# Linear attention into an MLP mixer on one core: every engine's order after the first batch taken from one written list

## The chip, the core and the metric

The kernel runs on one core of a Trainium2 chip. The core has a matrix engine (TensorE, PE in the profile, its weight loads PEld), three engines for elementwise work (VectorE or DVE, ScalarE or ACT, GpSimd or POOL) and SyncE (SP), which here only issues transfers. Every engine works off its own queue of instructions strictly in order; an instruction that waits holds up all that stands behind it on that engine, and nothing else. The metric is the device time of one execution in microseconds (us), lower is better.

## The reference

For each of 8 batches (8 heads, 576 positions, head size 64), attention without softmax, then a mixer over tokens and over channels:

```python
q_p, k_p = (phi(q), phi(k))                    # phi(x) = x + 1 for x > 0, else exp(x)
kv = np.einsum('bhsd,bhse->bhde', k_p, v)
z = np.sum(k_p, axis=2)
num = np.einsum('bhsd,bhde->bhse', q_p, kv)
den = np.einsum('bhsd,bhd->bhs', q_p, z)[..., None] + 1e-06
x = (num / den)                                # heads side by side: [batch, 576, 512]
h = np.maximum(xt @ w_tok1, 0.0) @ w_tok2      # xt: x with tokens last; 576 -> 256 -> 576
u = x + h.transpose(0, 2, 1)
out = u + np.maximum(u @ w_ch1, 0.0) @ w_ch2   # 512 -> 1536 -> 512
```

## The kernel before, in words

A batch's 576 positions are four blocks of 128 and a tail of 64. Operands are bf16, sums are kept in PSUM, eight banks of 128 x 512 f32. A batch n passes through these steps; the names in brackets are those that the changed kernel gives them, with the batch's number in front.

- SyncE loads q, k and v in halves (Lq0 to Lv1). phi takes three instructions a half: exp on ACT (kx, qx), the linear branch on DVE (ka, qa), the minimum of both on DVE (kb, qb). v is cast on ACT, in two halves of the first batches (1v0, 2v1) on DVE (v0, v1).
- TensorE forms kv (K); ACT copies it out (Kc0, Kc1). phi(q) is transposed, in batch 1 by TensorE (Q00 to Q11 with copies Qc), later by a transposing transfer on SyncE's queue (qT0, qT1). TensorE forms numerators and denominators (n); DVE divides (nd, ne, n0 to n2, o0, o1) into x.
- The token mixer is two matmuls (f0, f1 with ReLU on ACT; g0, g1 with the addition of x on DVE, gu0 and gu1). Its result u is transposed by a transfer (uT0, uT1), in batch 0 by TensorE (transposes of `utr_first`, copies on ACT and DVE).
- The channel mixer's first matmul has 12 chunks of the 1536 columns (m0 to m11, in batches 0 and 1 in halves ma and mb), each read out with ReLU (r). In batches 2 to 6 four of the 12 chunks, in batch 7 all, are done in seven products in place of eight (x21 to x27; y reads them), which needs sums of weight blocks (G21 to G24 in `swc`) and of u's blocks (s1 to s4).
- The second matmul is done in seven products too, for two halves of the positions each (p10 to p71), from row sums on DVE (w1 to w4) and weight sums (ws on GpSimd, wt on DVE); ACT holds partial results (c0 to c2), DVE adds u (eW to eZ), GpSimd adds the held parts (hY, hZ, hW) and issues the output's transfers (o). Batch 0 uses plain matmuls for it (q0 to q11, read by z). The tails of 64 positions go in pairs (gt, ut, T, U, V, W; in the last pair c, t and ts).

What sets the order before: the code walks through a list of TensorE pieces per batch (`big`), and a second list (`fill`) says after which piece which other step of this or of the following batches is emitted. The position in that emission is the position in the engine's queue. PSUM banks come from two rings in the first batch and from fixed numbers after it; output rows are staged in `obuf` by a running pointer (`o_slots`). Loads of later batches are held back by explicit waits: `load_all` passes the last transposing transfer as a gate.

Lines that matter below: L543 is the channel mixer's first matmul, L852 and L768 are the second one's products, L583 batch 0's second one, L712 and L740 the seven-product form of the first, L191 kv, L261 the numerators, L312 and L325 the token mixer, L202 TensorE's transposes of phi(q), L503 its transposes of batch 0's u, L521 and L526 the transposing transfers of u and of its tails, L157 and L165 phi on DVE, L176 the casts of v, L642 the weight sums on GpSimd, L700 the sums in `swc`, L610 the read of a tail's output, L861 and L863 the additions of u and of the held parts, L867 the output's transfers, L957 the load of `w_ch1` in four quarters of 384 columns (three chunks each), L798 and L834 the last batch's outputs.

In the first batch TensorE's pieces stand like this before:

```python
    utr_first([0], act)
    utr_first([1], dve)
    mm2_first(1, [2, 3])
    for mc in range(2):
        mm3(0, mc, range(0, 2))
    utr_first([2], act)
    utr_first([3], dve)
    for mc in range(2, 4):
        mm3(0, mc, range(0, 2))
```

Of the kernel before, what the change touches and what calls it, by code (L numbers as in the profile page):

```python
# [10 lines left out]
FP32 = mybir.dt.float32  # L11
# [4 lines left out]
EPS = 1e-6  # L16


@with_exitstack
def kernel(  # L20
# [20 lines left out]
    nc = tc.nc  # L41
# [22 lines left out]
    ring = {1: 0, 2: 0}  # L64

    def bank(at=None):
        if at is None:
            at, ring[1] = ring[1], (ring[1] + 1) % 4
        return psum[:, at]

    def banks(at=None):
        if at is None:
            at, ring[2] = 4 + ring[2], (ring[2] + 2) % 4
        return psum[:, at:at + 2]

    def two16():
        return banks().bitcast(BF16).rearrange("p a (t s) -> p a t s", s=128)
# [24 lines left out]
    uTj = [t.rearrange("p r j c -> p (r j c)").rearrange("p (j r c) -> p j r c", j=NDM, r=R) for t in uT]  # L102
    uTt = const("uTt", [128, 2, NDM, 128])
    cr = [const(f"cr{b}", [128, NCH, SM]) for b in range(2)]
    crt = const("crt", [128, NCH, 128])
    obuf = const("obuf", [128, 8, DM], FP32)
    swc = const("swc", [128, 4, 2, 256])
# [31 lines left out]

    live = {}  # L140
    o_at = [0]

    def o_slots(m):
        at = o_at[0] if o_at[0] + m <= 8 else 0
        o_at[0] = (at + m) % 8
        return obuf[:, at:at + m]

    def phi_exp(nm, n, j0, nj):
        f = raw[nm, rb(n)][:, j0:j0 + nj].rearrange("p j f -> p (j f)")
        e = work.tile([128, 2 * TD], BF16, name="e", tag="e", bufs=4)[:, :nj * TD]  # L150
        nc.scalar.activation(out=e, in_=f, func=AF.Exp)  # L151
        live["e", nm, n, j0] = e

    def phi_add(nm, n, j0, nj):
        f = raw[nm, rb(n)][:, j0:j0 + nj].rearrange("p j f -> p (j f)")
        y = work.tile([128, 2 * TD], BF16, name="y", tag="y")[:, :nj * TD]
        nc.vector.tensor_scalar(out=y, in0=f, scalar1=1.0, scalar2=1.0, op0=ALU.add, op1=ALU.max)  # L157
        for j in range(nj):
            live["y", j0 + j] = y[:, j * TD:]

    def phi_end(nm, n, j0, nj):
        c, i = divmod(j0, 2)
        dst = (kp if nm == "k" else qp)[:, c, :, i:i + nj]
        e, y = live["e", nm, n, j0], live["y", j0][:, :nj * TD]
        live["phi"] = nc.vector.tensor_tensor(  # L165
            out=dst.transpose([0, 2, 1, 3]), in0=e.rearrange("p (i t d) -> p i t d", i=nj, t=T),
            in1=y.rearrange("p (i t d) -> p i t d", i=nj, t=T), op=ALU.min)

    def phi(nm, n, c):
        phi_exp(nm, n, 2 * c, 2)  # L170
        phi_add(nm, n, 2 * c, 2)
        phi_end(nm, n, 2 * c, 2)

    def vcast(n, c, copy=nc.scalar.copy):
        js = slice(2 * c, 2 * c + 2)
        copy(out=vs[:, js, :, 0:D],  # L176
             in_=raw["v", rb(n)][:, js].rearrange("p j (t d) -> p j t d", t=T))

    def bank16():
        return bank().bitcast(BF16).rearrange("p (t s) -> p t s", s=128)  # L180
# [3 lines left out]
    def kv(n, cs):  # L184
        b = n % 2
        ps = banks(4 if n > 1 else None)[:, :, 0:2 * D1].rearrange(
            "p a (c e) -> p a c e", c=2)
        for c in cs:
            for t in range(T):
                for a, i in QUARTERS:  # L190
                    nc.tensor.matmul(out=ps[half[i], a, c], lhsT=kp[half[a], c, t, i],  # L191
                                     rhs=vs[half[a], 2 * c + i, t],
                                     start=(t == 0), stop=(t == T - 1))
        cs = slice(cs[0], cs[-1] + 1)
        for i in range(2):
            at = slice(i * D1, (i + 1) * D1)
            nc.scalar.copy(out=kvbd[b][half[i], cs, :, at].transpose([0, 2, 1, 3]),
                           in_=ps[half[i], :, cs])
# [6 lines left out]
    TS = [range(0, 5), range(5, T)]  # L205

    def qtr_put(n, c, ts, tp, put, dst=None):
        v_ = (qT[n % 2] if dst is None else dst)[:, 0:4 * TD].rearrange("p (a c t s) -> p a c t s", a=2, c=2, t=T)
        put(out=v_[:, :, c, ts[0]:ts[-1] + 1].transpose([0, 2, 1, 3]),
            in_=tp[:, 0:len(ts)].rearrange("p t (a s) -> p t a s", a=2))  # L210

    def qtr(n, c, put=nc.scalar.copy):
        tp = two16()
        for h, ts in enumerate(TS):
            qtr_mm(c, ts, tp[:, h])
        for h, ts in enumerate(TS):
            qtr_put(n, c, ts, tp[:, h], put)

    def qtr_dma(n, halves=range(2)):
        for a in halves:  # L220
            live["crossbar"] = nc.sync.dma_start_transpose(
                out=qT[n % 2][:, 2 * TD * a:2 * TD * (a + 1)].rearrange("p (f s) -> p f s", s=D),
                in_=qp[half[a]].rearrange("p c t i d -> p (c t i d)"))

    def nd_mm(n, c, rs):
        b = n % 2
        ps = banks()
        for s_, r in enumerate(rs):
# [5 lines left out]
        live["nd", c, rs[0]] = ps  # L234

    def nd_end(n, g, rs):
        b = n % 2
        m = len(rs)
        v_ = live["nd", g, rs[0]][:, 0:m, 0:HG * D1].rearrange("p r (h e) -> p r h e", h=HG)
# [9 lines left out]

    def nd_all(n):
        b = n % 2
        ps = [psum[:, 2 + 2 * m:4 + 2 * m] for m in range(3)]
# [10 lines left out]
        xv = x[b].rearrange("p r (c i a d) -> p i (r c) a d", c=2, i=2, a=2)  # L265
        v_ = [ps[m][:, :, 0:D1 * 7].rearrange("p i (k e) -> p i k e", k=7) for m in range(3)]
        dens = work.tile([128, 2, 2, 7], FP32, name="dens", tag="dens", bufs=1)
        last = work.tile([128, 2, 6], FP32, name="dens2", tag="dens2", bufs=1)
        both = psum[:, 2:6, 0:D1 * 7].rearrange("p b (k e) -> p b k e", k=7)
# [4 lines left out]
        def six(m, k0, rc0):  # L274
            den = (dens[:, m] if m < 2 else last)[:, :, k0:k0 + 6]
            nc.vector.tensor_tensor(  # L276
                out=xv[:, :, rc0:rc0 + 3],
                in0=v_[m][:, :, k0:k0 + 6, 0:D].rearrange("p i (q a) d -> p i q a d", a=2),
                in1=den.rearrange("p i (q a) -> p i q a", a=2)[
                    :, :, :, :, None].to_broadcast([128, 2, 3, 2, D]), op=ALU.mult)  # L280

        for m, at in enumerate((6, 0)):
            six(m, m, 4 * m)
            nc.vector.tensor_tensor(
                out=xv[:, :, 3, m], in0=v_[m][:, :, at, 0:D],
                in1=dens[:, m, :, at, None].to_broadcast([128, 2, D]), op=ALU.mult)
        nc.vector.tensor_scalar(out=last, in0=v_[2][:, :, 0:6, D], scalar1=EPS, scalar2=None,
                                op0=ALU.add)
        nc.vector.reciprocal(out=last, in_=last)
        six(2, 0, 7)  # L290

    def nd(n, g, rs):
        nd_mm(n, g, rs)
        nd_end(n, g, rs)

    ALL = slice(0, DM)
# [9 lines left out]
    def mm1(n):  # L306
        b = n % 2
        ps = banks(4 if n > 1 else None)
        for mt in range(NT):
            ms = slice(128 * mt, 128 * mt + 128)  # L310
            for r in range(R1):
                nc.tensor.matmul(out=ps[:, mt], lhsT=w1t[:, b, ms] if r == R else w1[:, r, ms],  # L312
                                 rhs=x[b][:, r, :], start=(r == 0), stop=(r == R))
        for mt in range(NT):
            nc.scalar.activation(out=ar[b][:, mt, :], in_=ps[:, mt], func=AF.Relu)

    def mm2(n, rs, add=False):

        b = n % 2
        m = len(rs)  # L320
        ps = bank().rearrange("p (a d) -> p a d", a=1) if n == 1 else banks(
            None if n < 2 else 4 if rs[0] else 6)
        for i, r in enumerate(rs):
            for kt in range(NT):
                nc.tensor.matmul(out=ps[:, i], lhsT=w2v(kt, r, b),  # L325
                                 rhs=ar[b][:, kt, :], start=(kt == 0),
                                 stop=(kt == NT - 1 and not add))
            if add:
                nc.tensor.matmul(out=ps[:, i], lhsT=identity, rhs=x[b][:, r, :], start=False,
                                 stop=True)  # L330
        if rs[0] == R:
            h = half[b]
            nc.vector.tensor_tensor(out=ut[n // 2 % 2][h], in0=ps[h, 0], in1=x[b][h, R], op=ALU.add)
        elif add:
            nc.scalar.copy(out=u[b][:, rs[0]:rs[0] + m], in_=ps[:, 0:m])
        else:
            nc.vector.tensor_tensor(out=u[b][:, rs[0]:rs[0] + m], in0=ps[:, 0:m],  # L337
                                    in1=x[b][:, rs[0]:rs[0] + m], op=ALU.add)

    def mm2_tails(p):  # L340

        ps = banks(6)[:, 0]
        for kt in range(NT):
            at = D * (T * kt + 2 * R)
# [966 lines left out]
```

## Time and profile before

| what | value |
|---|---|
| timed runs | 247.61 us median of 3 (247.29 to 248.21) |
| profiled execution, first to last instruction (span) | 246.4 us |
| profiled execution, its own time | not listed apart from the timed runs |
| TensorE busy | 236.1 us (96%) |
| VectorE busy | 198.8 us (81%) |
| ScalarE busy | 139.3 us (57%) |
| GpSimd busy | 76.9 us (31%) |
| TensorE clock granted | full in all 40 slices |
| transfers | 48.40 MB |

A busy share is an average over the span. For one step the question is which wait of TensorE ended last there, which the views of waits, of the chain and of the timeline tell. A row's duration is longer than the distance between two such rows that follow each other directly, since the engines overlap the end of one with the start of the next: 379 ns is the mean row of L543, and eight of them take 1.73 us in the chain, 0.216 us each.

### The profile page before, as it was taken

The page shows a single profiled execution, that of the slowest core. Times are in us where ns is not written, and L with a number is a line of the kernel's source. Part 1 is how long each engine was busy: PE and PEld are TensorE (multiplying, and loading weights), DVE is VectorE, ACT ScalarE, POOL GpSimd, SP SyncE. Part 2 cuts the span into 40 slices and gives each one's busy share as a digit, 9 for nine tenths or more (in the row PEclk, how much of TensorE's full clock was granted, in tenths as well). Part 3 has the DMA queues.
Part 4 walks back from the last instruction along what each step waited for, and adds up shares of the span by engine and source line. Part 5 has one row for each costly group of instructions (what it writes and reads, how often), then busy time and mean ns, then how long its engine had stood idle before and what let it go on. Part 6 is the DMA issues. An engine that isn't in the chain of part 4 may idle for free.

```text
span 246.4 us, 6090 instructions
## 1 busy us (share of the span) xinstructions
PE 236.1 (96%) x2477; PEld 162.3 (66%) x2496; DVE 198.8 (81%) x349; ACT 139.3 (57%) x224; POOL 76.9 (31%) x88
## 2 busy tenths in 40 slices
PE   7789999999999899999999999999999999999993
PEld 3475455564868456865678556865676567888883
DVE  5955877889799998988894499979996779956973
ACT  4673881569774367736897167656852652175100
POOL 9670030296703600061004500071007700440360
PEclk9999999999999999999999999999999999999999
DMA  6999999999726796589979955459748702352055
GB/s 248 267 203 258 348 275 308 355 251 289 294 24 133 223 334 271 132 224 210 358 263 174 412 148 192 93 115 329 228 89 94 170 3 43 64 112 61 4 127 130
DMA packets 50444, 48.40 MB, mean 196 GB/s; under 512 B 30192, under 2 KB 36720, under 8 KB 50416
## 3 DMA queue, kind: packets, MB, share of 16 engines
q1 hardware_dynamic: 41984, 35.00, 48.2%
q0 software_dynamic: 7472, 12.22, 22.7%
q10 hardware_dynamic: 960, 0.79, 1.4%
q8 instruction: 19, 0.31, 0.5%
q14 instruction: 9, 0.07, 0.1%
HBM read 35.85 MB, written 9.44 MB: 184 GB/s over the span
## 4 chain that ended last, share of the span: by engine, by line
PE 84%; DVE 6%; DMA 5%; issue 3%; ACT 1%; SPq 0%; DVEq 0%
PE ps L543 22%; PE ps L852 18%; PE ps L712 6%; PE ps L312 6%; PE ps L583 5%; PE ps L740 4%; PE ps L768 4%; PE ps L325 4%; DMA q_raw<-in_q_dram 3%; PE ps L557 2%; PE ps L570 2%; DMA uT<-u 2%; PE ps L820 2%; PE ps L261 2%; PE ps L191 1%
## 5 line engine op out<-in xcount | busy, mean ns | idle before, releaser
L543 PE MATMUL ps<-uT,wc 128*128 128x512 bf16 x252 | 60.2, 379 | 0.8 <-DMA uT<-u 0.5
L550 ACT ACTIVATE cr<-ps 128x512 bf16<-128x512 f32 x59 | 34.7, 600 | 32.9 <-PE ps L543 32.7
L543 PEld LDWEIGHTS <-wc 128*128 128x128 bf16 x256 | 24.1, 98 | 25.1 <-DMA uT<-u 0.8
L863 POOL TENSOR_TENSOR obuf<-obuf,q_raw 128x512 f32<-128x512 f32 x6 | 8.1, 1344 | 93.3 <-DVE obuf L861 59.1
L852 PE MATMUL ps<-k_raw,v_raw 128*128 128x256 bf16 x216 | 24.9, 273 | 0.0
L852 PEld LDWEIGHTS <-v_raw 128*128 128x128 bf16 x216 | 21.0, 98 | 3.9 <-issue 0.4
L852 PEld LDWEIGHTS <-cr 128*128 128x128 bf16 x216 | 21.1, 98 | 3.7
L861 DVE TENSOR_TENSOR obuf<-ps,u 128x512 f32<-128x512 f32 x24 | 16.3, 685 | 8.1 <-PE ps L852 5.8
L151 ACT ACTIVATE e<-q_raw 128x1152 bf16<-128x1152 f32 x16 | 18.3, 1163 | 7.3 <-DVE x L244 5.5
L151 ACT ACTIVATE e<-k_raw 128x1152 bf16<-128x1152 f32 x16 | 18.2, 1165 | 2.7 <-DMA k_raw<-in_k_dram 2.7
L852 PE MATMUL ps<-wc,cr 128*128 128x256 bf16 x144 | 17.7, 273 | 0.0
L276 DVE TENSOR_TENSOR x<-ps,dens 128x768 bf16<-128x768 f32 x18 | 17.2, 953 | 0.4
L655 DVE TENSOR_TENSOR v_raw<-cr 128x768 bf16<-128x768 bf16 (+2 forms) x24 | 14.8, 617 | 2.1 <-ACT cr L718 2.1
L337 DVE TENSOR_TENSOR u<-ps,x 128x1024 bf16<-128x1024 f32 x12 | 14.6, 1217 | 0.4 <-PE ps L325 0.3
L176 ACT CAST vs<-v_raw 128x1152 bf16<-128x1152 f32 x12 | 13.5, 1161 | 0.0
L312 PE MATMUL ps<-x,w 128*128 128x512 bf16 x49 | 13.0, 379 | 0.3
L165 DVE TENSOR_TENSOR qp<-e,y 128x1152 bf16<-128x1152 bf16 x16 | 11.9, 753 | 1.6 <-ACT e L151 0.9
L165 DVE TENSOR_TENSOR kp<-e,y 128x1152 bf16<-128x1152 bf16 x16 | 12.7, 816 | 0.5 <-ACT e L151 0.4
L157 DVE TENSOR_SCALAR y<-k_raw 128x1152 bf16<-128x1152 f32 x16 | 11.7, 763 | 1.3 <-DMA k_raw<-in_k_dram 1.3
L157 DVE TENSOR_SCALAR y<-q_raw 128x1152 bf16<-128x1152 f32 x16 | 12.4, 793 | 0.4 <-DMA q_raw<-in_q_dram 0.4
L325 PE MATMUL ps<-ar,w2p 128*128 128x512 bf16 x44 | 11.8, 379 | 0.3
L583 PE MATMUL ps<-wc,cr 128*128 128x512 bf16 x47 | 11.9, 379 | 0.1
(182 smaller groups left out, 458.8 us busy)
## 6 DMA issues: line engine op xcount, KB each, us to landing
k_raw<-in_k_dram SPq DMA_DIRECT2D x16, 576.0 KB, 7.6
q_raw<-in_q_dram SPq DMA_DIRECT2D x16, 576.0 KB, 5.9
v_raw<-in_v_dram SPq DMA_DIRECT2D x14, 576.0 KB, 9.2
out_dram<-obuf POOLq DMA_DIRECT2D x12, 512.0 KB, 6.9
wc<-in_moe_w_ch_dram POOLq DMA_DIRECT2D x8, 384.0 KB, 9.8
out_dram<-obuf POOLq DMA_DIRECT2D x4, 256.0 KB, 6.0
out_dram<-obuf ACTq DMA_DIRECT2D x12, 64.0 KB, 2.2
out_dram<-obuf SPq DMA_DIRECT2D x12, 64.0 KB, 1.9
```

What stands on the lines that cost most here:

```text
L151: nc.scalar.activation(out=e, in_=f, func=AF.Exp)
L157: nc.vector.tensor_scalar(out=y, in0=f, scalar1=1.0, scalar2=1.0, op0=ALU.add, op1=ALU.max)
L165: live["phi"] = nc.vector.tensor_tensor(out=dst.transpose([0, 2, 1, 3]), in0=e.rearrange("p (i t d) -> p i t d", i=nj, t=T), in1=y.rearran ...
L276: nc.vector.tensor_tensor(out=xv[:, :, rc0:rc0 + 3], in0=v_[m][:, :, k0:k0 + 6, 0:D].rearrange("p i (q a) d -> p i q a d", a=2), in1=den.r ...
L312: nc.tensor.matmul(out=ps[:, mt], lhsT=w1t[:, b, ms] if r == R else w1[:, r, ms], rhs=x[b][:, r, :], start=(r == 0), stop=(r == R))
L325: nc.tensor.matmul(out=ps[:, i], lhsT=w2v(kt, r, b), rhs=ar[b][:, kt, :], start=(kt == 0), stop=(kt == NT - 1 and not add))
L543: nc.tensor.matmul(out=ps, lhsT=wc1[:, kj, 128 * mc:128 * mc + 128], rhs=uTj[b][:, kj] if n < 2 else uT[b][:, :, kj], start=(kj == 0), sto ...
L550: nc.scalar.activation(out=cr[b][:, mc, :], in_=ps, func=AF.Relu)
L583: nc.tensor.matmul(out=ps, lhsT=crt[:, kc, :] if t == 8 else cr[b][:, kc, 128 * r:128 * r + 128], rhs=wc2[:, kc, :], start=(kc == 0), stop ...
L655: return engine.tensor_tensor(out=s_[which - 1][:, ks], in0=x_, in1=y_, op=op)
L852: nc.tensor.matmul(out=live[tile_][:, j], lhsT=lhs[:, k_], rhs=rhs[:, k_], start=(first and j == 0 and k_ == 0), stop=(k_ == KH - 1), skip ...
L861: nc.vector.tensor_tensor(out=o, in0=live[tile_], in1=u[n % 2][:, d::2, HC[c]], op=ALU.add)
```

## The change

The emission by `big` and `fill` is gone. Every step becomes a named closure (`put`), a table `BANK` gives each PSUM tile its bank, `SLOT` each staged output its rows of `obuf`, `EBUF` and `YBUF` each phi its buffers, `GATE` the loads that wait for a transfer, and one list `ORDER` of names is worked off at the end. The steps that were one are split where the list puts other work between the parts (the seven divisions of `nd_all`, the four sums of `group_sums`, matmul and read). The instructions on TensorE are the same in number and shape, and each step stays on its engine. Up to the last piece of batch 0's token mixer (A43) the order is that of before; from there on it is another in all queues.

In batch 0 two halves of a chunk (0ma1, 0ma0) stand around one transpose each (At2, At3), and the chunks come in the order 1, 0, 5, 7, 4, 10 and so on. The loads of one batch lie among those of the next, and those of batch 4 are no longer all held until u's transfer of batch 2 has landed. The products p come in a freer order, `swc` is summed in four places, and the last batch's products alternate with the rest of batch 6.

```diff
--- before.py
+++ after.py
+GATE = {'1k0': ('wc1', 0), '2q0': ('wc2', 1), '4q0': ('u', 2, 1), '7q0': ('u', 5, 1)}
+
+ON_DVE = {'1v0', '2v1', '0r3', '0r6', '0r9', '1r5', '1r8'}
...
+BANK = {k_: int(v_) for k_, v_ in (e.split(":") for e in """2K:2 2n0:2 2n1:4 2n2:6 2f:2 2g0:2 2g1:0 2X2:0 2Z2:4 2Y2:1 2gt:6 3K:3 3n0:2 3n1:4 3n2:6 3f:5 3g0:2 3g1:6 3X2:1
...
+SLOT = {k_: int(v_) for k_, v_ in (e.split(":") for e in """0o0:0 0o1:2 1P:4 V0:0 2P:1 3P:0 V1:4 4P:0 5P:4 6P:0 7P0:4 7t:6 7P1:0""".split())}
...
+ORDER = """A2 A0 A1 A3 A4 A5 A6 A8 A9 A7 A10 A12 A13 A14 A11 A16 A17 A15 A19 A18 A21 A20 A22 A23 A24 A25 A26 A27 A28 A29
+A30 A33 A31 A32 A35 A34 A36 A37 A38 1Lk0 A39 1Lk1 1Lq0 A40 1Lq1 A41 1Lv0 A42 A43 1Lv1 0ma1 At2 0ma0 At3 0ma5
+0ma7 0ma4 0mb1 0mb7 0mb5 0r7 0mb4 0r5 0mb0 0r1 0ma10 0gt 0mb10 1kx0 0gv 0ma2 1ka0 0ma3 0r0 0ma9 0r4 0mb9 0r10
+0ma11 0r9 0ma6 1kx1 1ka1 0mb11 0ma8 G21 0mb8 0r11 1kb1 0mb3 0r8 B0 1kb0 1qx0 0q1 B1 1qa0 0mb2 1qa1 1qx1 B2
+0mb6 1qb0 0q0 0r2 1qb1 1Q00 1Q01 1v0 1Qc00 0q2 0r3 1Qc01 1v1 0r6 1Q10 1Q11 1K 1Qc11 1Qc10 1Kc1 1Kc0 0q3 2Lq0
+ws02 2Lq1 1n00 2Lk1 1n01 ws04 1nc00 0q4 2Lv0 0q5 1nc01 1n10 0q6 1nc10 1n11 ws14 0q7 1nc11 1n20 0q8 ws12 1nc20
+1n21 2qx0 0q9 1nc21 1f0 2qa0 2qa1 3Lq0 0q10 1fr0 2Lk0 2qb0 2qx1 2Lv1 1f1 2qb1 0q11 1fr1 0z0 2kx1 2qT1 ws00
...
+2kb1 1mb4 1r7 1mb8 ws20 1r10 2K 1r8 1r4 1ma9 2Kc0 3qa1 2Kc1 1mb9 ws32 2n 1r9 3qx1 2nd T00 0o1 2o1 2o0 1ma11
+2ne Tr00 2n1 1mb11 T02 ws30 1r11 2n2 1p10 2n0 T01 3qa0 2f0 1w10 1w20 2f1 2fr0 3qb1 1w13 1p11 2fr1 1w23 U00
+Tr02 3qb0 Tr01 2g0 3kx1 3ka0 3qT1 U01 2gu0 3v0 3qT0 1p50 3ka1 1c0 2g1 3v1 2uT0 1w30 1p61 1w40 1p60 1p51 2gu1
+1c1 1p20 1c2 3kb1 1p71 2uT1 3kx0 1p21 4Lk1 1p70 1eZ 4Lv0 U02 1eW 4Lk0 3kb0 1p31 4Lq0 2s3 1p41 2s1 4Lq1 1p40
+1p30 1eX 2m1 1eY G22 3K 2r1 1hY V0 2m0 3Kc1 3Kc0 1hZ 3n 2r0 4v0 3nd 2m3 1hW 3o0 3n0 2m2 2r3 5Lv0 3ne 4Lv1 2x21
...
+5p10 5r7 6fr1 5w10 5p11 5y24 5w20 6g1 5c0 7qb1 7v0 6g0 5w13 7qT0 5w23 5p20 7v1 6gu0 5p61 7qT1 5p60 6gu1 5p21
+6uT0 5c1 5p50 5w30 6uT1 5p51 5eZ 7K 5c2 5w40 5p71 7Kc0 7Kc1 5p70 5p31 5eW 5p30 5p40 5eY 5p41 5hY 7n 5eX 6m0
...
+7R11 7t6 7D701 7R21 7p40 7D210 7t5 7D200 7R40 7R30 7tb2 7D700 7p61 7tr6 7D301 7tr5 7D400 7t7 7D401 7t3 7D211
+7tr7 7tr2 7p51 7td70 7td71 7R61 7tr3 7D300 7t4 7td21 7R51 7td30 7p71 7td31 7tr4 7td20 7p31 7td41 7R71 7td40
+7D711 7p41 7R31 7D710 7D311 7D310 7R41 7D411 7D410"""
...
-    ring = {1: 0, 2: 0}
-
-    def bank(at=None):
-        if at is None:
-            at, ring[1] = ring[1], (ring[1] + 1) % 4
-        return psum[:, at]
...
+    def bank(name):
+        return psum[:, BANK[name]]
...
+    tok = {}
+
+    def put(name, fn, *a):
+        assert name not in tok, name
+        tok[name] = lambda: fn(*a)
+
     live = {}
...
+    def load_in(nm, n, c):
+        gate = GATE.get(f"{n}{nm}{c}")
+        live["in", nm, n, c] = load(nm, n, c, live[gate] if gate else None)
...
+    for name in ORDER.split():
+        tok[name]()
```

In `ORDER`, 7D and 7td are the last batch's output transfers; their last digit says which queue issues them, 0 for SyncE, 1 for ScalarE.

## The prediction

> **What bounds the kernel now.** I read the engines' busy shares first, then the 40 slices.
>
> ```profile
> PE 236.1 (96%) x2477; PEld 162.3 (66%) x2496; DVE 198.8 (81%) x349; ACT 139.3 (57%) x224; POOL 76.9 (31%) x88
> PE   7789999999999899999999999999999999999993
> ```
>
> TensorE bounds it: its row is full but for the first slices and the last. The matmuls are the same after the change, so a new order can gain only what TensorE idles from 21 us on, where the orders part. The waits of TensorE give that:
>
> ```profile
> PE ps L261 <- DVE obuf L610: 0.6, 1, 0.6
> PE ps L543 <- DMA uT<-u: 0.5, 1, 0.5
> PE ps L543 <- issue: 0.2, 1, 0.2
> ```
>
> These are in total, times, longest. From one start to the next they cost TensorE 0.69 us (at 85.50), 0.66 us (at 189.61) and 0.2 us (at 61.3): together 1.55 us. All other waits of TensorE lie before 21 us. The chain that ended last shows what stood before the two long ones (start, us, what):
>
> ```profile
> 82.59 1.04 DVE swc L700
> ...
> 86.30 1.83 PE ps L543 x8
> ...
> 184.38 5.18 DMA uT<-u
> 189.61 1.90 PE ps L543 x8
> ```
>
> The timelines of VectorE and GpSimd around the first show why `swc` was late:
>
> ```profile
> 78.91 2.49 DVE L165 TENSOR_TENSOR kp<-e,y 128x1152 bf16<-128x1152 bf16 x2
> 82.52 1.11 DVE L700 TENSOR_TENSOR swc<-wc 128x512 bf16<-128x512 bf16 x1
> ```
>
> ```profile
> 79.07 1.71 POOL L863 TENSOR_TENSOR obuf<-obuf,q_raw 128x512 f32<-128x512 f32 x1 [0.59 <-DVE obuf L861]
> 82.08 1.27 POOL L863 TENSOR_TENSOR obuf<-obuf,w 128x512 f32<-128x512 f32 x1 [1.29 <-DVE obuf L861]
> ```
>
> One of the two kp rows takes 1.82 us and the first swc row 1.11, where their like take 0.75 and 0.42 beside no GpSimd row: 1.76 us late here, some 3.8 us of VectorE over the whole run. Of that 0.69 reached TensorE.
>
> **What the change removes.** Its orders put the swc sums in four places, none of them beside a GpSimd addition, and issue uT1 of batch 6 without a qT right behind it. I take all three stalls as gone: **-1.55 us** (bounds -1.55 and -0.9: the 0.66 stays if that transfer again finds company). The other 3.1 us of VectorE are hidden behind full TensorE slices: nothing. Steps that change place with TensorE still fed cost nothing while what feeds them is early; the thinnest covers that I found by adding row spacings (a row's duration less 0.08 us on VectorE, 0.11 on ScalarE, 0.216 us per 512-column matmul) are: batch 2's division, 3.9 us of VectorE behind 4.2 us of matmuls (T00, m11, T02, p10, T01); batch 6's, 3.9 behind 3.5, whose lack of 0.4 the queued matmuls before it, two banks ahead, can bear; uT in batches 3 to 7, wanted 4.5 to 7.4 us after its issue for the usual 3.1. If such a cover fails, the lack itself is the price. Batch 2's k and v loads now pass Lq0 of batch 3 on SyncE and are issued near 47 us, not 38; wanted at 58.5 and landing in 7.6 us by their page row, they keep 4 us. GpSimd's weight sums stand earlier or keep over ten TensorE pieces before their reader (ws30 and 1p41); output 5o is issued near 219 us, and its staged rows are wanted again near 230.
>
> **What it adds.** In batch 0 TensorE now gets to several pieces earlier than their inputs. Rows of before:
>
> ```profile
> 21.86 0.61 PE L503 MATMUL ps<-identity,u 128*128 128x128 bf16 x8
> 22.30 2.32 PE L543 MATMUL ps<-uT,wc 128*128 128x512 bf16 x10
> ...
> 36.14 0.82 PE L191 MATMUL ps<-vs,kp 64*64 64x65 bf16 x72
> ```
>
> ```profile
> 21.02 0.69 DVE L486 TENSOR_TENSOR u<-ps,x 128x512 bf16<-128x512 f32 x1
> ```
>
> ```profile
> 35.25 1.18 ACT L176 CAST vs<-v_raw 128x1152 bf16<-128x1152 f32 x1
> ```
>
> ```profile
> DMA to landing us min/median/max: 9.7/10.4/13.5
> ```
>
> - (a) The transpose At2 reads the u that VectorE finishes at 21.71. Before, four matmuls of `w_ch1` stood ahead of it and it ran at 21.86; now two do (0ma1), ending at 21.43. **+0.3** (0 to 0.4). Behind At2 the whole queue of TensorE waits.
> - (b) 0ma10 needs the last quarter of `w_ch1`. GpSimd issued it at 13.16 and it took 13.5 us (the last line above, of L957's four transfers): it lands at 26.67. Before, chunk 9 was reached at about 29.9. Now ten half chunks stand ahead of 0ma10, and from 21.43 with the transposes and (a) it is reached at 22.6 + 8 x 0.432 = 26.05. **+0.6** (0 if it lands after the median 10.4, to 1.0). 0gt and 0mb10 wait behind.
> - (c) 1Q00 needs 1qb0, the last of a chain on VectorE that starts with 0r9's wait for 0mb9 at about 30.1: r9 0.60, ka1 0.67, G21 0.34, kb1, kb0, qa0, qa1, qb0 at 0.67 each give 35.1 to 35.3; TensorE is there at 35.1. **+0.2** (0 to 0.5).
> - (d) 1K needs v's second half, cast on ScalarE behind the two copies 1Qc00 and 1Qc01, which wait for 1Q00 and 1Q01: 35.65 + 0.57 + 0.48 + 1.06 + 0.11 = 37.9, where TensorE wants it at 37.5. **+0.4** (0 to 0.8). Before, the cast ended at 36.43, in the kv row's own 0.82.
> - (e) Loads for batch 4: before, they were issued from 81.5 on, when uT1 of batch 2 had landed. Now three halves (4Lk1, 4Lv0, 4Lk0) follow it on SyncE at once, near 78.9, and only 4Lq0 waits. Its reader is m1 of batch 2 at about 83.8, 5.4 us after the issue. Alone such a transfer takes 3.1 us, at worst 5.2, and its like for the tails up to 10.8:
>
> ```profile
> DMA to landing us min/median/max: 3.0/3.1/5.2
> ```
>
> ```profile
> DMA to landing us min/median/max: 2.4/8.1/10.8
> ```
>
>   (The first line is of L521, the second of L526.) At 5.2 the matmul itself is not late; the row sums 2s3 and 2s1, which VectorE now does ahead of the read 1eX, are, and 3K waits for that read's bank: 0.4. At 8.1 it costs 2.7. The loads stand behind the transfer in the queue, not ahead of it as at the 8.1 row, so I take between the first two: **+0.2** (0 to 2.7).
> - (f) The end. SyncE's last twelve outputs are issued in the written order, some behind a reading that comes later than their own:
>
> ```profile
> 241.83 1.76 SPq L798 DMA_DIRECT2D out_dram<-obuf  x3
> ```
>
>   Three in 1.76 us, issues 0.645 apart. By the new order 7td70 waits for 7tr7 at about 239.55 and seven more follow: the last is issued 0.3 to 0.65 behind its data. **+0.35** (0 to 0.65).
>
> Sum: 0.3 + 0.6 + 0.2 + 0.4 + 0.2 + 0.35 = 2.05, minus 1.55: **+0.5 us**. The execution shown spans 246.4; the median of the runs is 247.61, so 1.2 us lie around the span, and I carry them over. 246.9 + 1.2 = **248.1 us**. A timing of this kernel can't tell less than some 0.5% (1.24 us) from no change: 246.37 to 248.85.
>
> **A page against the rows, for the first stall.** The Trainium skill, "SBUF — State Buffer", section "Who interferes with whom", says that a VectorE instruction with two SBUF inputs and a GpSimd instruction that reads SBUF exclude each other, the later one being blocked fully. The rows agree (1.82 us beside 0.75). By the page alone, moving all such rows would be worth the 3.8 us they lost, and the sum would read 245.0; the waits show that TensorE felt 0.69 of them.
>
> **A page against the change.** The Trainium skill, "DMA: Bandwidth & Descriptors", section "Issuing engines are not separate DMA queues", says that transfers run on the same 16 engines and interleave whoever issues them. By it a transpose moved from outputs to loads has only changed its company; the tails' 10.8 us beside loads and outputs and 2.4 alone say as much, and the sum at 8.1 for (e) would be 250.6.
>
> **The rivals.**
>
> - *Faster: the waits of batch 0 don't come.* For: (a) to (d) are each under 0.7 us, made of row spacings that may be 2% off over 14 us, and (b) hangs on one slow landing of four. Against: the landing in (b) is a measured 26.67, and k's and v's loads crowd it as before. Then only 0.3 of (f) is left: 246.4 - 1.55 + 0.3 + 1.2 = 246.35. 0.14.
> - *Slower: a transposing transfer among loads lands late.* Place: 2uT1 at 78.4. Price: landing less 5.4 us, so it decides from 5.4 on; at 8.1 the sum gains 2.5: 250.6. For: three 576 KB loads issued within 2 us behind it, and the tails' two late landings. Against: uT1 at 130.94 had q's loads 1.5 us behind it and still took 5.2; the most that a uT took. The like holds for uT of batch 7, with 4.5 us. 0.24.
> - *Slower: VectorE's and ScalarE's chain into batch 1 lags.* If (a) to (d) all come at their upper ends, 2.7 in place of 1.5, and (f) too, the end is at 249.6. For: (c) and (d) hang on each other. Against: four upper ends at once. 0.12.
> - *The change does little at all:* new stalls as small as the old, which is the forecast's own low side: -1.55 + 0.7 gives 246.8. In the forecast's chance.
>
> **How the numbers follow.** Forecast 0.50, its own range 246.8 to 249.0; nearly all of it within 0.5%, 0.04 above. The faster rival lies on the bound: 0.12 of its 0.14 faster. Both slower rivals lie above 248.85. So faster 0.12, same 0.48, slower 0.40. The range runs from the faster rival's time to the late transfer's, 246.4 to 250.6; beyond these lie half of the faster rival and a part of the late transfer, some 0.2.
>
> **What would show it.** Right: no wait at the numerators of batch 3 and at batch 6's first chunk; waits of L503 for VectorE near 21.4, of L543 for a transfer into `wc` near 26, of L202 and L191 near 35 to 38; uT1 of batch 2 landing within 5.4 us. Wrong: TensorE without gaps from 21 to 40 (faster), or a wait of L543 for uT above 1 us, or a VectorE row of 1 us and more ahead of a TensorE wait in a later batch (slower). I would be wrong altogether if a bank or a staged row that I did not follow ties two engines where before they were free.

## The result, and the profile after

The changed kernel takes 249.03 us (median of 6 runs, 248.75 to 249.76), the kernel before 247.46 us (6 runs). The ratio is 1.0064, 95% interval 1.0048 to 1.0080: slower by 1.57 us, where 248.1 was forecast. The time lies inside the range, and beyond the 0.5% that I had called within the noise: it is the outcome to which I had given 0.40.

The engines' busy shares and the slices of the changed kernel look like those of before, and the clock granted to TensorE is full until its last matmul, at 242.99. TensorE is still the bound; the span, 247.5 us, is 1.1 us longer than the one shown before:

```profile
PE 237.4 (96%) x2478; PEld 162.7 (66%) x2496; DVE 198.0 (80%) x349; ACT 138.2 (56%) x224; POOL 76.6 (31%) x88
PE   7899999999999999999999999999999999999992
```

The waits of TensorE in the changed kernel (total, times, longest; L673 is the first matmul, L734 batch 0's second one, L289 kv):

```profile
PE ps L673 <- DVE x L400: 0.6, 1, 0.6
...
PE ps L673 <- DMA wc<-in_moe_w_ch_dram: 0.3, 1, 0.3
...
PE ps L734 <- ACT cr L682: 0.3, 1, 0.3
PE ps L289 <- DVE cr L680: 0.2, 1, 0.2
```

Neither of the two long waits of before is in the list; four others are. The first is in batch 6 (below). The places of the other three, and of one at 21.04 that is too short for the list, in the timeline of TensorE:

```profile
21.04 0.63 PE L633 MATMUL ps<-identity,u 128*128 128x128 bf16 x4
...
26.10 0.60 PE L673 MATMUL ps<-uT,wc 128*128 128x512 bf16 x2 [0.32 <-DMA wc<-in_moe_w_ch_dram]
...
32.36 1.02 PE L734 MATMUL ps<-wc,cr 128*128 128x512 bf16 x3 [0.25 <-ACT cr L682]
...
37.43 0.77 PE L289 MATMUL ps<-vs,kp 64*64 64x65 bf16 x71 [0.25 <-DVE cr L680]
```

The bracket gives idle time after the modelled end of the row before. From start to start, less the row's own spacing, these waits cost more: 0.23 us at 21.04 (four transposes take 0.63, where eight took 0.61 before), 0.48 at 26.10, 0.42 at 32.36, 0.46 at 37.43. Together 1.59 us in batch 0 and at the door of batch 1. The last one follows two reads of banks on VectorE (0r3 and 0r6):

```profile
36.10 1.28 DVE L680 TENSOR_SCALAR cr<-ps 128x512 bf16<-128x512 f32 x2
```

The wait in batch 6 costs 0.75 us from start to start. The chain that ended last names what it followed:

```profile
190.83 0.96 DVE x L400
192.95 2.06 DVE crt L872
195.22 0.88 DVE x L400
196.14 1.02 PE ps L673 x4
```

The `crt` row (6s1) is one of u's sums in SBUF. The timelines of VectorE and of GpSimd show it at 2.15 us, where its like take 0.42, beside an addition on GpSimd:

```profile
192.87 2.15 DVE L872 TENSOR_TENSOR crt<-uT 128x512 bf16<-128x512 bf16 x1
```

```profile
192.16 1.28 POOL L1060 DMA_DIRECT2D out_dram<-obuf  x2
193.45 1.28 POOL L1056 TENSOR_TENSOR obuf<-obuf,part 128x512 f32<-128x512 f32 x1
```

That is the stall of before in another batch. By row, less the usual row of its shape, the VectorE rows that work from SBUF lost some 4.9 us after the start, where the kernel before lost some 3.8: a little more, and in other places. The end is the last part: TensorE ended 4.46 us before the span's end, 3.80 in the kernel before. SyncE's last outputs:

```profile
240.05 0.71 SPq L976 DMA_DIRECT2D out_dram<-obuf  x1
240.86 1.86 SPq L1022 DMA_DIRECT2D out_dram<-obuf  x3
242.82 1.83 SPq L976 DMA_DIRECT2D out_dram<-obuf  x3
```

From 240.05 on they are issued back to back, the last at 244.11; its data was ready at 243.45, when VectorE's last addition ended:

```profile
243.03 0.42 DVE L971 TENSOR_TENSOR obuf<-ps,u 128x256 f32<-128x256 f32 x1 [0.25 <-PE ps L957]
```

### The profile page after: what moved, and what is told of

Read it like the earlier page. It is cut to its first block, busy times and chain, and to the rows that moved or that the text cites. A ratio compares the mean times of both kernels' runs of the same rounds, so it can differ in the third digit from the quotient of the medians.

```text
span 247.5 us, 6061 instructions
## 1 busy us (share of the span) xinstructions
PE 237.4 (96%) x2478; PEld 162.7 (66%) x2496; DVE 198.0 (80%) x349; ACT 138.2 (56%) x224; POOL 76.6 (31%) x88
## 4 chain that ended last, share of the span: by engine, by line
PE 81%; DMA 9%; DVE 6%; POOL 2%; issue 1%; POOLq 0%; DVEq 0%
PE ps L957 26%; PE ps L673 18%; PE ps L915 10%; PE ps L435 6%; DMA wc<-in_moe_w_ch_dram 5%; PE ps L734 5%; PE ps L446 4%; DMA cr<-in_v_dram 3%; PE ps L698 2%; PE ps L720 2%; PE ps L289 2%; PE ps L1010 2%; PE ps L374 2%; DVE crt L872 1%; DVE y L243 1%
## 5 line engine op out<-in xcount | busy, mean ns | idle before, releaser
L673 PE MATMUL ps<-uT,wc 128*128 128x512 bf16 x252 | 61.0, 379 | 1.1 <-DVE x L400 0.6
L682 ACT ACTIVATE cr<-ps 128x512 bf16<-128x512 f32 x59 | 33.8, 601 | 33.9 <-PE ps L673 32.5
L673 PEld LDWEIGHTS <-wc 128*128 128x128 bf16 x256 | 24.1, 98 | 24.9 <-issue 1.4
L1056 POOL TENSOR_TENSOR obuf<-obuf,w 128x512 f32<-128x512 f32 x6 | 7.9, 1313 | 88.4 <-DVE obuf L1049 88.4
L957 PE MATMUL ps<-k_raw,v_raw 128*128 128x256 bf16 x252 | 31.9, 273 | 0.0
L957 PEld LDWEIGHTS <-cr 128*128 128x128 bf16 x252 | 24.5, 98 | 5.2
L957 PEld LDWEIGHTS <-v_raw 128*128 128x128 bf16 x252 | 24.5, 98 | 4.6 <-issue 0.4
L957 PE MATMUL ps<-wc,cr 128*128 128x256 bf16 x168 | 21.9, 273 | 0.1
L400 DVE TENSOR_TENSOR x<-ps,dens 128x768 bf16<-128x768 f32 x18 | 16.5, 943 | 0.1
L439 ACT ACTIVATE ar<-ps 128x512 bf16<-128x512 f32 x14 | 8.4, 601 | 8.7 <-PE ps L435 8.7
L243 DVE TENSOR_SCALAR y<-q_raw 128x1152 bf16<-128x1152 f32 x16 | 13.2, 833 | 0.0
L734 PE MATMUL ps<-wc,cr 128*128 128x512 bf16 x46 | 12.0, 379 | 0.4 <-ACT cr L682 0.3
```

The costliest lines, as they stand in the source:

```text
L243: nc.vector.tensor_scalar(out=ybuf[YBUF[f"{n}{nm}{c}"]], in0=f, scalar1=1.0, scalar2=1.0, op0=ALU.add, op1=ALU.max)
L400: nc.vector.tensor_tensor(out=xv[:, :, rc0:rc0 + 3], in0=nd_tile(n, m)[:, :, k0:k0 + 6, 0:D].rearrange("p i (q a) d -> p i q a d", a=2), i ...
L673: nc.tensor.matmul(out=bank(f"{n}m{mc}"), lhsT=wc1[:, kj, 128 * mc:128 * mc + 128], rhs=uTj[b][:, kj] if n < 2 else uT[b][:, :, kj], start ...
L682: nc.scalar.activation(out=o, in_=ps, func=AF.Relu)
L734: nc.tensor.matmul(out=bank(f"U{p}{t}"), lhsT=crt[:, kc, :] if t == 8 else cr[b][:, kc, 128 * r:128 * r + 128], rhs=wc2[:, kc, :], start=( ...
L957: nc.tensor.matmul(out=ps, lhsT=lhs[:, k_], rhs=rhs[:, k_], start=(first and not skip and k_ == 0), stop=(k_ == KH - 1), skip_group_check= ...
```

## The experiments

In all of them the line numbers are one less than in the changed kernel, except in the two made from the kernel before. "TensorE's stretch" is the time from the first L673 (L672, L543) to the end of the last matmul: 221.64 us in the execution of before that the prediction used, 222.38 in the changed kernel.

### Batch 0 in its old order

```diff
-0ma1 At2 0ma0 At3 0ma5 0ma7 0ma4 0mb1 0mb7 0mb5 0r7 ... 0r3 1Qc01 1v1 0r6 1Q10 1Q11 1K
+0ma0 0ma1 At2 At3 0ma2 0ma3 0mb0 0r0 0mb1 0r1 0mb2 0r2 0gt 0gv ... 0q2 1Q10 1Q11 1K
```

> The changed kernel with batch 0's channel mixer, phi of batch 1 and the transposes up to 1K in the order of the kernel before (and banks to suit). Theory 1, the waits of TensorE add up: the four waits that the changed kernel's trace shows between 21 and 38 us (0.24 for u, 0.49 for w_ch1, 0.42 for the read 0r8, 0.46 for the read 0r6) go, and nothing later takes them: 1.6 us less than the changed kernel, about 247.4. Theory 2, batch 1 is bounded by VectorE and the loads, and the waits only move on: less than 0.8 us gained, and new waits of TensorE between 38 and 85 us.

The edit also gives nine of batch 0's chunks the PSUM banks that fit this order. (The new order starts inside batch 0, behind its token mixer, and not after the batch as the title says.)

Measured: 248.03 us (12 runs), ratio to before 1.0020 (1.0010 to 1.0031); 1.0 us less than the changed kernel. TensorE's stretch fell by 1.39 us to 220.99, in an execution 0.26 us below its median against one 0.24 above, and no wait came between 38 and 190 us. The waits left behind 21 us are that of batch 6 and 0.22 us inside kv. So the waits of batch 0 were a loss on the path and theory 1 holds, with 1.0 to 1.4 us in place of 1.6: kv's 0.22 is also in the kernel before (0.21 in its second trace, below, though not in its first), and the wait for `w_ch1` differs between executions, as the next runs show.

### One GpSimd row away from 6s1

```diff
-5eY 5p41 5hY 7n 5eX ... 6r1 7n1 5hW 6m8
+5eY 5p41 5hW 5hY 7n 5eX ... 6r1 7n1 6m8
```

> The changed kernel with one GpSimd row moved: 5hW (an addition in SBUF) ahead of 5hY, so that it runs at about 188 us and not at 193.45, beside the VectorE sum 6s1. Theory 1, the GpSimd row held 6s1 (2.15 us in place of 0.42) and by it 6m2: the row falls to 0.8 us or less, the wait of 0.75 us at 195.4 goes, about 248.3. Theory 2, the issuing of output 4o beside it (192.16 to 193.44) or uT's landing held 6s1: the row stays above 1.5 us and the wait stays, 249.0.

Timelines of VectorE, then of GpSimd:

```profile
192.45 0.43 DVE L871 TENSOR_TENSOR crt<-uT 128x512 bf16<-128x512 bf16 x1
```

```profile
191.73 1.28 POOL L1059 DMA_DIRECT2D out_dram<-obuf  x2
193.02 0.68 POOL L855 TENSOR_TENSOR k_raw<-wc 128x256 bf16<-128x256 bf16 x1
```

The row took 0.43 us, all of it beside the issuing of 4o, and the wait in batch 6 is gone from the list. So the addition held it and the issuing did not: theory 1. Timed: 248.64 us (9 runs, 247.88 to 249.11), 0.4 less than the changed kernel by the medians and 0.6 by the ratios to the kernel before (1.0040 and 1.0064), where 0.75 was expected; both kernels still carry the wait for `w_ch1`, which spreads their runs over more than a microsecond.

### The last outputs in the order of their data

```diff
-7D701 7R21 7p40 7D210 7t5 7D200 7R40 ... 7tr3 7D300 7t4 7td21 7R51 7td30 ... 7tr4 7td20
+7D200 7D701 7R21 7p40 7D700 7D210 7t5 7R40 ... 7D211 7D301 7tr5 7D400 7D300 ... 7td20 7td30
```

> The changed kernel with the last outputs issued in the order in which VectorE finishes their data (7D200 first, 7D300 ahead of 7td70, 7td20 ahead of 7td30, 7D211 ahead of 7D301). Theory 1, SyncE's queue at 0.65 us an output sets the end: its last issue falls from 0.65 us behind its data to under 0.1, 0.65 us less, about 248.4. Theory 2, ScalarE's queue, whose last landing comes only 0.28 us earlier, then sets it: 0.3 less, 248.7.

SyncE's last outputs:

```profile
236.38 3.04 SPq L975 DMA_DIRECT2D out_dram<-obuf  x4
240.39 2.43 SPq L1021 DMA_DIRECT2D out_dram<-obuf  x4
243.04 1.76 SPq L975 DMA_DIRECT2D out_dram<-obuf  x3
```

The last is issued at 244.34, 0.03 us behind its data. From TensorE's end to the span's end it is 3.78 us, as in the kernel before (3.80), where the changed kernel has 4.46: 0.68 less. Timed 248.32 us (12 runs), 0.7 less by the medians, 0.5 by the ratios; with this spread the times alone would not part the two theories, the trace does: theory 1. The same run shows the wait for `w_ch1` at its longest:

```profile
26.96 0.60 PE L672 MATMUL ps<-uT,wc 128*128 128x512 bf16 x2 [1.26 <-DMA wc<-in_moe_w_ch_dram]
```

The quarter landed at 26.91 here, and TensorE lost 1.42 us from start to start; in the run before this one it landed at 25.53 and TensorE lost nothing. The 12 times fall into two groups, seven from 247.95 to 248.37 and five from 249.25 to 249.43; the trace is of one of the five.

### The three together

> The three edits together. Theory 1: the gains add, 1.6 + 0.75 + 0.65 = 3.0 us less than the changed kernel, 246.0, which is 1.4 us (0.6%) less than the kernel before. Theory 2: the later batches stall where the earlier waits are gone, 247.0 or more.

Measured: 246.45 us (7 runs, 246.34 to 246.71), ratio to before 0.9956 (0.9939 to 0.9972): 2.6 us less than the changed kernel and 1.0 less than the kernel before, faster than both. TensorE's stretch is 220.13 us, and of its waits between 21 us and the end one is left, 0.20 us at 36.84 for a later load of weights into `wc`. The profile's first lines:

```profile
span 244.7 us, 6065 instructions
## 1 busy us (share of the span) xinstructions
PE 236.5 (97%) x2478; PEld 162.8 (67%) x2496; DVE 196.4 (80%) x349; ACT 138.3 (57%) x224; POOL 76.8 (31%) x88
```

The gains add, to within 0.4 us of the 3.0 expected, and the median lies 0.45 above the 246.0. What the new order behind batch 0 was worth, then, is about this 1.0 us, 0.7 of it the wait near 85 us; its part from 21 to 38 us, the order of its last outputs and the place of one GpSimd row cost 2.6.

### The wait for `w_ch1` alone

```diff
-0mb0 0r1 0ma10 0gt 0mb10 1kx0 0gv 0ma2 1ka0 0ma3 0r0 0ma9 0r4
+0mb0 0r1 0gt 1kx0 0gv 0ma2 1ka0 0ma3 0ma10 0r0 0ma9 0mb10 0r4
```

> The changed kernel with 0ma10 and 0mb10 alone moved behind 0ma3 and 0ma9, so that the last quarter of w_ch1 is wanted about 1.4 us later, near 27.1. Theory 1, the landing of that quarter (25.4 to 26.9 in the executions seen) sets a wait of 0 to 1.4 us that differs from execution to execution: the wait is gone in every execution, the timed runs lie within 0.5 us of each other where the changed kernel's lie 1 to 1.5 us apart, and the median is 0.5 us less, near 248.5. Theory 2, it only moves to the reads behind it: 249.0 and the spread stays.

Measured: 248.63 us (5 runs, 248.53 to 248.85). The wait is gone, TensorE's stretch is 221.92 (0.46 less), and the spread is 0.3 us in 5 runs, where it was 1.0 in 6. Theory 1: the order of before reached that quarter at 29.9 us and so never saw when it landed; the new one reads it at the moment it lands.

### (a) alone

```diff
-0ma1 At2 0ma0 At3
+0ma1 0ma0 At2 At3
```

> The changed kernel with 0ma0 put ahead of At2, so that four matmuls stand ahead of the transposes as in the kernel before. Theory 1, (a) and (b) are one wait: the 0.24 us at u go, but the last quarter of w_ch1 lands when it lands, and the wait for it grows by as much; from the first chunk to 0mb10 TensorE is no earlier. Theory 2, they are two: 0.24 us gained, whatever the landing.

Measured: 249.11 us (one run). The 0.23 us at the transposes are gone, and the next wait in TensorE's timeline is

```profile
25.96 0.61 PE L672 MATMUL ps<-uT,wc 128*128 128x512 bf16 x2 [0.48 <-DMA wc<-in_moe_w_ch_dram]
```

0.48 idle in place of 0.32, with a quarter that landed 0.08 us sooner after the first chunk than in the changed kernel. TensorE's stretch is 222.31, 0.07 less, as much as the quarter landed sooner. Theory 1: (a) and (b) are one wait, until the quarter lands.

### The reads behind it

```diff
-0mb3 0r8 B0 1kb0 1qx0 0q1 B1 1qa0 0mb2
+0mb3 0r8 B0 1kb0 1qx0 0mb2 0q1 B1 1qa0
```

> The changed kernel with 0mb2 ahead of 0q1, which covers the wait of 0.42 us for 0r8. Theory 1, VectorE is the bound from 30 to 37 us (0r9 to 0r6 back to back), so that 1K waits 0.4 us longer instead: 0.8 to 0.9 us, no gain. Theory 2, the waits are separate: 0.42 us gained, the wait of 1K stays at 0.46.

Measured: 248.92 us (one run), TensorE's stretch 222.22. Both theories missed. 0q1 no longer waits, kv's wait is as before, and 0.42 us turned up between the two:

```profile
34.60 0.66 PE L306 MATMUL ps<-identity,qp 128*128 128x128 bf16 x9 [0.26 <-ACT cr L681]
```

```profile
37.07 0.77 PE L288 MATMUL ps<-vs,kp 64*64 64x65 bf16 x71 [0.24 <-DVE cr L679]
```

1Q00's bank is read out by 0r2 on ScalarE, which stands behind both exponentials of q and ends at 34.54. The wait moved from one read on ScalarE to the next. 1qb0, which the prediction had followed to this place, ends at 34.49: by that it alone would have held 1Q00 nearly as long. The 0.16 us gained on the changed kernel is what `w_ch1` cost less here (0.31 for 0.48).

```diff
-1qb0 0q0 0r2 1qb1 1Q00 1Q01 1v0 1Qc00 0q2 0r3 1Qc01 1v1 0r6
+1qb0 0q0 0r2 0r6 1qb1 1Q00 1Q01 1v0 1Qc00 0q2 0r3 1Qc01 1v1
```

> The changed kernel with the read 0r6 on VectorE ahead of 1qb1, so that 1K finds its bank free. Theory 1 (step d of the prediction was right behind it): 1K then starts at once, and its second half waits for 1v1's cast on ScalarE, 0.3 to 0.4 us; no gain of more than 0.15 us. Theory 2, only the bank held 1K: its wait of 0.46 us goes and nothing takes its place.

Measured: 249.27 us (one run), and again neither. VectorE's timeline, then TensorE's:

```profile
36.01 0.75 DVE L261 CAST vs<-v_raw 128x1152 bf16<-128x1152 f32 x1
36.68 0.68 DVE L679 TENSOR_SCALAR cr<-ps 128x512 bf16<-128x512 f32 x1
```

```profile
37.41 0.78 PE L288 MATMUL ps<-vs,kp 64*64 64x65 bf16 x72 [0.40 <-DVE cr L679]
```

kv needs two banks, and the other one waits for 0r3, which is now the last of the same chain. VectorE is busy from 29.5 to 37.3 us with twelve steps; whichever of them stands last holds kv until 37.4. In the same execution VectorE had stood idle for 4.7 us up to 27.3, when the old order had started 0r3 at 25.9 and 0r6 at 29.4 (in the trace of the first experiment). That is where the 0.46 us come from: reads that the new order puts late. With both reads early, as in the first experiment, 0.22 us of it stay, for the cast of v.

### Loads ahead of a transposing transfer

```diff
-3kb1 1p71 2uT1 3kx0 1p21 4Lk1 1p70 1eZ 4Lv0 U02 1eW 4Lk0
+3kb1 1p71 4Lk1 4Lv0 4Lk0 2uT1 3kx0 1p21 1p70 1eZ U02 1eW
```

> The changed kernel with 4Lk1, 4Lv0 and 4Lk0 issued ahead of uT1 of batch 2, not behind it. Theory 1, loads in flight ahead of a transposing transfer delay it, loads issued behind it do not: uT1 lands 5 to 8 us after its issue, not 3.1, and m1 of batch 2 waits 0 to 2.7 us. Theory 2, loads as company cost a transposing transfer nothing: 3.0 to 3.5 us.

Measured: 253.1 us (one run). SyncE's timeline, then TensorE's:

```profile
78.25 0.91 SPq L214 DMA_DIRECT2D v_raw<-in_v_dram  x1
79.22 0.46 SPq L214 DMA_DIRECT2D k_raw<-in_k_dram  x1
79.77 1.65 SPq L475 DMA_TRANSPOSE uT<-u  x1
```

```profile
85.83 1.04 PE L672 MATMUL ps<-uT,wc 128*128 128x512 bf16 x4 [1.62 <-DMA uT<-u]
...
88.17 0.77 PE L288 MATMUL ps<-vs,kp 64*64 64x65 bf16 x71 [1.05 <-DVE obuf L1048]
```

The transfer took 6.01 us from issue to landing, and it was issued at 79.77 where the changed kernel issues it at 77.91; there, with the same three loads behind it, it took 3.12. Theory 1, with one execution of each order. It cost 1.79 and 1.27 us at these two places, the second by 1eX behind the row sums; of the other 1.0 us of the 4.1 that this run took more, 0.7 are the wait for `w_ch1`, 1.16 here.

### The kernel before, once more

> The kernel before once more, for a second trace. Theory 1, the late landing of uT1 of batch 6 (5.18 us) belonged to the execution shown, whose span was longer than most: it lands in 3.1 to 4 us here, the wait of 0.66 us is not there, and only the one of 0.69 at 85.5 was there to be gained; span about 245.6. Theory 2, it is the rule: 5.2 us and the wait again, span 246.4.

Measured: 247.26 us (one run), span 245.5. The transfer at 184.09 landed in 3.34 us and TensorE did not wait for it. The wait near 85 is there again:

```profile
85.18 0.79 PE L261 MATMUL ps<-kvbd,qT 64*128 64x65 bf16 x40 [0.63 <-ACT cr L550]
```

Theory 1. TensorE's stretch is 221.19 us here. (This time the wait is put down to a read on ScalarE that ends at 85.18, just as the numerators start; V0's read on VectorE ends at 85.03. The next experiment tells which of the two it was.)

### The swc sums alone, in the kernel before

```diff
+    put(9, group_sums)
...
-    put(28, group_sums)
```

> The kernel before with one part of the change alone: the four swc sums moved from batch 1's end, where a GpSimd row stands beside them, to VectorE's idle time near 61 to 63 us. Theory 1, they held the read of V0 and with it the numerators of batch 3: the wait of 0.7 us near 85 us goes, 246.8. Theory 2, the read on ScalarE that ends at the same moment (the second trace of the kernel before names it) sets that wait: it stays, 247.5.

Measured: 250.67 us (6 runs), ratio 1.0104 (1.0081 to 1.0128). Both halves of the story are in one trace. The wait near 85 us is gone: the numerators start at 88.86, while the read on ScalarE ends at 89.56. So the sums did hold V0's read (theory 1). But the idle time into which I had moved them was beside GpSimd's weight sums, in one group of six from 58.47 on (VectorE's timeline, GpSimd's, then the longest wait of TensorE):

```profile
60.77 0.78 DVE L700 TENSOR_TENSOR swc<-wc 128x512 bf16<-128x512 bf16 x1
61.59 1.27 DVE L700 TENSOR_TENSOR swc<-swc,wc 128x512 bf16<-128x512 bf16 x1
62.78 1.38 DVE L700 TENSOR_TENSOR swc<-wc 128x512 bf16<-128x512 bf16 x1
64.08 1.38 DVE L700 TENSOR_TENSOR swc<-wc,swc 128x512 bf16<-128x512 bf16 x1
```

```profile
58.47 8.01 POOL L642 TENSOR_TENSOR q_raw<-wc,q_raw 128x512 f32<-128x512 bf16 x6 [1.91 <-DVE kp L165]
```

```profile
PE ps L557 <- DVE x L284: 2.6, 1, 2.6
```

They took 4.8 us in place of 1.7, pushed the division of batch 2 back, and TensorE waited 2.6 us for its bank. The edit did by itself what the change did in batch 6.

The wait is not the whole loss of 3.1 us. Right behind it the clock granted to TensorE falls to a half, from 67.23 to 70.64, which no other trace here has before TensorE's last matmul. The matmuls of L557, of which 32 follow, start 0.107 us apart in place of 0.056, 1.6 us more (the profile's row of the clock, then TensorE's timeline):

```profile
PEclk9999999999889999999999999999999999999999
```

```profile
67.16 3.54 PE L557 MATMUL ps<-uTt,wc 128*128 128x128 bf16 x32 [2.55 <-DVE x L284]
```

The trace is of the slowest of the six runs. Four have a mean clock of 0.990 to 0.993 and take 250.62 to 250.91 us; the two at 0.998 and 0.999 take 249.53 and 249.68.

## Why the prediction was right, and where it was wrong

The forecast's mechanism, old waits swapped for new ones in batch 0 and at the end, is what happened. Its sum was 1.07 us short, and several terms were right for the wrong reason. The outcome given 0.40 came, but not by the rival that held most of it (the late transfer, 0.24): the time passed 248.85 by a stall counted as a gain that most executions don't have, and by batch 6, which stood at nothing. The sign that the prediction gave for slower, a VectorE row of 1 us and more ahead of a TensorE wait in a later batch, is the one that came.

| step | forecast | measured |
|---|---|---|
| stalls removed | -1.55 | -0.70, and two small ones |
| (a) the u of At2 | +0.3 | 0.23, part of (b) |
| (b) last quarter of `w_ch1` | +0.6 (0 to 1.0) | 0.48 here; 0 to 1.42 |
| (c) 1Q00 for 1qb0 | +0.2 | 0; in its place 0q1 for 0r8, 0.42 |
| (d) 1K for v's cast | +0.4 | 0.46, for 0r6 |
| (e) uT1 with loads behind | +0.2 | 0: it landed in 3.1 us |
| (f) the last outputs | +0.35 (0 to 0.65) | 0.66 |
| batch 6's division | 0 | +0.75 |

**What was removed** was the largest miss. Of the three stalls only the one at 85 us was there to be gained. The 0.66 us at 189.61 belonged to the execution shown, whose span of 246.4 was long: the second trace has 245.5 and no such wait. Every timed run of the later sets takes 1.7 to 1.95 us more than its span (249.27 for 247.5, 247.26 for 245.5), so the execution shown was, by that, the run of 248.21, not one of 247.61, and "1.2 us lie around the span" set a long execution against a median. The 0.2 us at 61.3 were no wait at all. From start to start it is 0.351 us there, where the same switch of shape takes 0.125 at 82.86. The 0.226 us between are about one 512-column spacing of 0.216, and the chunk behind them shows three matmuls where it has four: a matmul whose record is missing. The same gap stands in the changed kernel at 134.3, also behind a kv, and is in none of the three traces that have all 2496 matmuls.

**Between two traces** the sum closes. From the second trace of before to the changed kernel's, TensorE's stretch grew by 222.38 - 221.19 = 1.19 us. The new waits are 1.59 + 0.75 = 2.34; gone are 0.70 at 85 us, 0.21 inside kv, and five gaps of about 0.045 at the first product of each mixed group, 1.14 in all; that leaves 1.20. The end adds 0.64, and the first chunk of the channel mixer starts 0.12 later. The medians differ by 1.57, less than these together, since the changed kernel's trace is of a run 0.24 above its median and that of before of one 0.2 below.

**(a), (b)**: the reasoning stood, the bound was too narrow. Its upper end took the landing of 26.67 as about the worst; it was 26.91 in an execution in which TensorE began the channel mixer earlier (20.54, where it is 21.00 in the trace used). The two terms are one wait, up to the landing, as the experiment on (a) alone shows; since (b)'s arrival included (a), their sum counted it once.

**(c), (d)**: about the right size, wrong instruction. I followed phi and the cast, and of the reads that free banks I followed none: 0r8 for 0q1, then 0r2 for 1Q00, 0r3 and 0r6 for kv. The prediction had said that a bank not followed would make it wrong; it was the banks. That (a) to (d) came to 1.6 us for the 1.5 forecast is in part luck, but the instructions followed stood close behind the reads: 1qb0 ended 0.06 us before 0r2, and the cast of v 0.28 us after 0r6 (37.66 and 37.38 in the changed kernel). That a backlog of VectorE and ScalarE would hold TensorE at this place was right; it is the mechanism of the rival with the lagging chain, at the forecast's price.

**Batch 6**: "the queued matmuls before it can bear" the lack of 0.4 us. VectorE's rows there lost 0.38 and 1.73 us more, beside GpSimd; of these 2.11 us the matmuls bore 1.36, and 0.75 came through. The step failed because I took spacings of undisturbed rows for a stretch in which the change puts GpSimd's 7F12, 4o and 5hW, and looked at the swc sums alone for such neighbours. The Trainium skill, "SBUF — State Buffer", section "Who interferes with whom", has a VectorE instruction with two SBUF inputs contend with a GpSimd instruction that reads SBUF; the runs agree, 2.15 us beside the addition and 0.43 beside the issuing of an output.

**(e)** and the rival of the late transfer: the condition was "landing over 5.4 us", and it is met only with the loads ahead: 6.01 us there, 3.12 with them behind. The page set against the change, the Trainium skill's "DMA: Bandwidth & Descriptors", section "Issuing engines are not separate DMA queues", makes no difference between the two. Here the measurement decides: the loads behind the transfer cost it nothing in this place. That loads behind never do is not shown; the transfer at 130.94 of the kernel before took 5.19 us with loads behind it, but had two other transposing transfers just ahead. The rival's price was right for the case that did not come: 3.06 us at the two places.

**(f)** had the right mechanism and the middle of its bounds; the end takes the whole 0.65. The span ends 1.35 to 1.36 us after SyncE's last landing, in the kernel before, in the changed one and in the one with the outputs reordered, whether ScalarE's last landing comes 0.28 us before it (the changed kernel) or 0.28 to 0.31 after it (the other two). The faster rival fell with batch 0's waits, which came.

## What to carry to other kernels

A new order is judged at the points where the old one had slack to spare: list for every matmul that moves forward the load, the bank's last read and the operand it now meets first, and say for each when that is there. Waits that follow each other up to one late arrival are one wait, and taking away an early one only lengthens the last. Before a stall in a trace is counted as a gain, hold that trace's own time against the other runs and look for the stall in a second one.

## What the runs showed of the hardware

- The same transfer of `w_ch1` landed between 25.4 and 26.9 us in the thirteen executions traced, all with the same orders up to its issue: nine times by 26.05, four times from 26.63 on. With an order that reads it at that moment, 12 runs fell into two groups of times 1 us apart; 5 runs of one that reads it 1 us later lay within 0.3 us.
- A sum of VectorE in SBUF that starts 0.6 us ahead of the recorded start of a GpSimd addition was still held by it (6s1 at 192.87, the addition at 193.45). Whether the record of the GpSimd row begins late, or the VectorE row had not begun, stays open.
- A transposing transfer took 6.0 us with three loads issued in the 2.1 us ahead of it and 3.1 us with the same loads behind it (one execution each).
- A wait of TensorE of 2.55 us was followed by 3.4 us at half the clock, 1.6 us more on top of the wait. The wait of 1.6 us in the experiment on the loads was followed by none.
